# Attention, mixing layer and top-2 attention experts in one kernel: float32 exponentials for the first six pairs of heads

## The chip, the cores and the metric

One core of a Trainium2 chip runs the whole kernel in one launch. The metric is device time in microseconds (us), from the profiler, median of several executions; less is better. The engines are TensorE (PE for matrix products, PEld for its weight loads), VectorE (DVE), ScalarE (ACT), GpSimd (POOL) and SyncE (SP, which issues nearly all DMAs).

## The reference, cut to what matters

Three layers follow each other, for 4 batches, sequence 576, 8 heads of 64. Only the first, a decayed causal attention, and the start of the second are touched.

```python
scores = q @ k.T / 8 + cum[:, None] - cum[None, :]    # cum: running sum of log f; causal
attn = exp(scores - rowmax); attn /= attn.sum(-1) + 1e-9
x = attn @ v                                          # per head, laid out [batch, 576, 512]
u = x + (x.T @ U @ V).T                               # second layer
y = u + relu(u @ w_ch1) @ w_ch2
# third layer: four single-head attention experts over y, two of them chosen for each token
```

## The kernel before, in words

**Stages.** The attention stage handles 32 heads in 16 pairs (a pair is 128 of the 512 columns of x). It is followed by a dense stage (the products with w_ch1 and w_ch2, quarter by quarter of the weights) and by the stage of the experts. Some products of the dense stage's first quarter (the fills) are already mixed into the attention stage, from pair 5 on: PER_PAIR (line 45) says how many for each pair, and none belongs to pairs 0 to 4.

**Order.** The attention stage is a list of events, each with a due time: `put(h, us, do)` puts an event at `us` microseconds into the slot of head h (SLOT = 8.4), `early` puts it into the 15.6 before slot 0. The list is sorted by due time and issued in that order, and PE, DVE, ACT, POOL and SP each keep their part of that order (line 1299). The due times order the work; they don't time it.

**One head.** head_events (line 962) issues two sets of score products into two PSUM tiles (float32r, L267), exponentials of both on ACT (L287, three pieces of 576, 512 and 512 columns), a copy of each piece to float16 on ACT (high_part, L292) and the remainder to float16 on DVE (low_part, L295). One slot later (due at 4.55) `attend` multiplies: weighted_values (L323, L325, L327) takes 15 blocks of 128x128, each with three float16 products (high exponential with high v, high with low v, low with high v), with a column of ones behind v that yields the row sums. row_scales (L372, L375) and normalise (L389) on DVE finish the head.

**Row maxima.** max_events (line 996) runs two heads ahead: in the slot of head h PE makes the rows of head h+2 (last_rows L184 into `ua`, first_rows_of L202 into `ub`), DVE takes maxima (last_max L189, then first_max L210 in four pieces), and in the next slot PE turns them (turn_max L216), ACT scales them (put_row L222) and a DMA puts them as row 127 into the head's q (L226). Score tiles, `ua` and `ub` share two PSUM buffers (tag s2) in the order: first scores, second scores, ua, ub.

**Values.** value_events (line 1033) reads v of a pair (load_v L818, one DMA), finds a power of two near its largest value (L333, L338, L345 to L347, L353, L358) and splits v into float16 high (ACT, L362) and low (DVE, L365).

**Filler products.** `busy` (line 1255) issues products of a constant with itself (L1258) that nobody reads: 8, 14 and 8 of them in each slot of heads 0 to 9.

**Other work in the slots.** split_high, split_moves and split_low (lines 820 to 862) cut q and k of a pair into high and low parts, two pairs ahead; the second head's halves are moved between partitions by DMA. mix_events (line 1116) makes u of a finished pair in odd slots: mix_sums (L873, plain float32 products), a copy on ACT (L877), mix_low on DVE (L880), two turns on PE (L890, L892), a copy and a store of u to DRAM (L897, L921). Weights of the first quarter are unpacked in slots 4 to 13.

**Before slot 0.** FIRST_SPLITS (line 1082) gives the due times of the splits of pairs 0 and 1; the moves of head 0 and the load of pair 1 stand ahead of the moves of head 1.

**Start of the dense stage.** For batches 1 and 2, ffn_begin (line 606), ffn_begin_high and ffn_begin_low fetch and cut u in the attention stage. For batch 3, `ffn_prepare(NC * (B - 1))` (line 1369) runs at the start of the dense stage: a DMA reads u (L629), ACT and DVE cut it (L652, L653).

Of the kernel before, what the change touches and what calls it, by code (L numbers as in the profile page):

```python
# [42 lines left out]
SLOT = 8.4  # L43
FIRST = 15.6
PER_PAIR = (0,) * 5 + (3, 3, 3, 3, 4, 4, 4, 4, 3, 3, 2)

# [18 lines left out]
def kernel(  # L65
# [44 lines left out]
    nc.gpsimd.memset(every[:], 1.0)  # L110
    spread = const.tile([P, P], BF16, name="spread")
    nc.gpsimd.memset(spread[:], 1.0 / VEXP)
    ars = []
# [123 lines left out]
    def exponent_tiles(pl_, n, eng=nc.gpsimd):  # L237

        made = []
        for i in range(n):  # L240
            two = pl_.tile([P, 2 * 1600 + 64], F16, name=f"ph{i}")
            eng.memset(two[:, 3200:3264], 0.0)
            made.append((two, two[:, 1600:3264]))
        return made
# [52 lines left out]
    def scores(hb, exps, select=False):  # L297

        ph, pl = exps
# [12 lines left out]
        return ph, pl  # L312

    def weighted_values(ph, pl, vh, vl, its=(0, NT), av=None):
# [26 lines left out]
    def value_power(at_):  # L341
# [3 lines left out]
        nc.vector.tensor_reduce(ar, at_[:], AX.X, OP.max)  # L345
        nc.vector.tensor_scalar(ar, ar, 1.0e-30, None, OP.max)
        nc.vector.tensor_scalar(ar.bitcast(I32), ar.bitcast(I32), 0x7F800000, None,  # L347
# [3 lines left out]
    def value_spread(full):  # L351
        rp = psf.tile([P, 1], F32, name="rsp", tag="f")
        nc.tensor.matmul(rp[:], spread[:], full[:].bitcast(BF16)[:, 1:2], start=True, stop=True)  # L353
        return rp
# [13 lines left out]
    def row_scales(av, rs):  # L368

        den = small.tile([P, NT], F32, name="den")  # L370
        total = av()[:, :, 64:65].rearrange("p t o -> p (t o)")
        nc.vector.tensor_scalar(den[:], total, 1.0e-9 * PSCALE, rs()[:, 0:1], OP.add, OP.mult)  # L372
        yield
# [425 lines left out]
    khigh = att.tile([P, S], F32R, name="khigh")  # L799
    vhs = []  # L800
    for i in range(2):
        vh_ = hpool.tile([P, 2, NT, 65], F16, name=f"vh{i}")
        vl_ = hpool.tile([P, 2, NT, 64], F16, name=f"vl{i}")
        nc.vector.memset(vh_[:, :, :, 64:65], 1.0)
        vhs.append((vh_, vl_))
    NPAIR = B * NP
# [26 lines left out]
    def split_moves(p, j):  # L833

        if p >= NPAIR:
            return
        qa, qb, ka, kb = pair_heads(p)[j]
        src = f32(chl[2 * p + j:2 * p + j + 1]) if p < 2 else cdram[2 * p + j]
        nc.sync.dma_start(f32(ka[64:66, 0:S]), src)
        if p == j == 0:  # L840
            load_qk(1)
        if j == 0:
            nc.sync.dma_start(f32(qb[lo_, :]), f32(qa[lo_, :]))
            nc.sync.dma_start(f32(kb[hi_, :S]), f32(ka[lo_, :S]))
        else:
            nc.sync.dma_start(f32(qa[lo_, :]), f32(qb[hi_, :]))
            nc.sync.dma_start(f32(ka[lo_, :S]), f32(khigh[hi_, :]))
            nc.sync.dma_start(f32(kb[lo_, :S]), f32(khigh[hi_, :]))

# [112 lines left out]
    def head_events(h):  # L962

        p, j = divmod(h, 2)
        hb = pair_heads(p)[j]
        ph, pl = exps[h % 2]
        st = {}
# [4 lines left out]
        def exp_(n):  # L972
            u, view = (0, 0) if n == 0 else (1, n - 1)
            view, o0, n_, _ = score_views(st[u], u)[view]
            st["pf", n] = exponentials(view, n_), o0, n_
# [9 lines left out]
        def attend():  # L985
            vh, vl = vhs[p % 2]
            st["av"] = weighted_values(ph, pl, vh[:, j], vl[:, j])

        put(h + 1, 4.55, attend)
        finish = row_scales(lambda: st["av"], lambda: st_rs[p])  # L990
        for us in (6.15, 6.35):
            put(h + 1, us, lambda: st.update(rn=next(finish)))
        put(h + 1, 6.55, lambda: normalise(places[p % 2][2][:, :, j * D:j * D + D], st["av"],
                                           st["rn"]))

    def max_events(h):
# [13 lines left out]
        if h < 2:  # L1010
            for us, n in ((8.5, 0), (8.7, 1)) if h == 0 else ((12.3, 0), (13.2, 1)):
                early(us, rows, n)
            early((9.2, 12.9)[h], lambda: last_max(st[0], st["mx"]))
            for n, t in enumerate((3, 2, 1, 0)):
                early((9.8, 13.7)[h] + 0.6 * n, first, t)
        else:
# [16 lines left out]
    def value_events(p):  # L1033
# [11 lines left out]
        vh, vl = vhs[p % 2]  # L1045
        if p == 0:
            early(6.6, step, "am", None, value_max)
            early(11.7, step, "amt", "am", value_turn)
            early(13.9, step, "full", "amt", value_power)
            early(14.9, step, "rp", "full", value_spread)  # L1050
            put(0, 0.2, factor)
            put(0, 4.95, lambda: value_high(vr, st_rs[p], vh))
            put(0, 8.0, lambda: value_low(vr, st_rs[p], vh, vl))
            return
        put(h, 1.95, step, "am", None, value_max)
        put(h, 4.54, step, "amt", "am", value_turn)
# [6 lines left out]
    def split_events(p):  # L1063
# [15 lines left out]
        put(2 * (p - 2) - 1 if p > 2 else 0, 0.1, load_qk, p)  # L1079
        put(2 * (p - 2), 2.0 if p > 2 else 8.1, load_v, p)  # L1080

    FIRST_SPLITS = ((5.8, 6.5, 7.5), (7.1, 8.8, 10.3), (11.6, 14.7, 14.8), (13.2, 19.3, 19.2))

    def first_events():
# [5 lines left out]
        def table():  # L1090
            one_ = small.tile([1, 1], F32, name="one", bufs=1)
            nc.scalar.activation(one_[:], vhs[0][0][0:1, 0, 0, 64:65], AF.Ln)

# [191 lines left out]
    put(10, 4.6, read_late)  # L1285
    for b in (1, 2):
        put(8 * b + 8, 4.0, ffn_begin, b)
# [592 lines left out]
```

## Time and profile before

| | us |
|---|---|
| median of 3 runs (819.69 to 822.27) | 821.81 |
| the profiled execution | 822.43 |
| its span, from the first to the last instruction | 820.4 |
| PE busy in the span | 765.5 (93%) |
| DVE busy | 626.0 (76%) |
| ACT busy | 450.6 (55%) |
| mean granted TensorE clock | 0.991 |

Busy time is a union of intervals: a PE that is busy by the table can still be issuing slower than it could. "Idle before" in a row is the time in which the engine did nothing ahead of that instruction, with what ended it. In a row of the timeline, several like instructions in sequence are merged: the first number is the start, the second the time to the end of the last one.

### The profile page before, as it was taken

The numbers are of one execution on the slowest core, as the hardware profiler recorded it, in microseconds if no ns is written. First come the engines' busy times: TensorE is split into PE (matmuls) and PEld (weight loads), VectorE is DVE, ScalarE is ACT, GpSimd is POOL, SyncE is SP. The second block draws the span as 40 slices with busy tenths as digits, with TensorE's granted clock in tenths as the row PEclk, the third lists the DMA queues.
The fourth block names the chain that finished last, engine by engine and source line by source line (L and its number), as shares of the span: only waits on it lengthen the run. The fifth ranks groups of instructions, "written<-read, shape, count | busy, mean of one in ns | idle before, by whom it ended". The sixth has DMA issues, their size and how long they took to land.

```text
span 820.4 us, 19717 instructions
## 1 busy us (share of the span) xinstructions
PE 765.5 (93%) x7726; PEld 659.4 (80%) x7726; DVE 626.0 (76%) x1716; ACT 450.6 (55%) x895; POOL 148.3 (18%) x248
## 2 busy tenths in 40 slices
PE   3898889999999989998999999999999999889997
PEld 2788889999999989876777777777778887768764
DVE  6899999999999839979773685467436798877874
ACT  6778887877787615627231232113212666566674
POOL 9542433324232000000010000000001411010110
PEclk9999999999999999999999999999999999989999
DMA  6466665666564154854033234200101433122222
GB/s 187 133 188 177 179 194 147 188 185 172 168 173 131 58 168 152 278 161 157 34 116 97 79 95 160 81 1 1 59 30 37 124 96 91 43 76 57 51 82 81
DMA packets 59212, 96.10 MB, mean 117 GB/s; under 512 B 4928, under 2 KB 39088, under 8 KB 59120
## 3 DMA queue, kind: packets, MB, share of 16 engines
q1 hardware_dynamic: 56864, 90.78, 37.3%
q10 hardware_dynamic: 2256, 4.06, 1.4%
q8 instruction: 61, 1.00, 0.5%
q14 instruction: 31, 0.25, 0.1%
HBM read 53.25 MB, written 23.74 MB: 94 GB/s over the span
## 4 chain that ended last, share of the span: by engine, by line
PE 46%; DVE 7%; issue 2%; DMA 2%; ACT 1%; POOL 0%; SPq 0%; POOLq 0%
PE cps L678 15%; PE hps L662 14%; PE pq L1522 4%; PE pv L1574 3%; PE po L1608 3%; PE sc L267 2%; PE ub L202 1%; DMA yst<-ydram 1%; DVE ph L295 1%; PE av L323 1%; PE av L327 1%; DVE ub L210 1%; DVE w16a L519 1%; PE av L325 1%; DMA ust<-udram 1%
## 5 line engine op out<-in xcount | busy, mean ns | idle before, releaser
L667 ACT ACTIVATE hh<-hps 128x288 f16<-128x288 f32 (+1 forms) x128 | 52.6, 411 | 218.4 <-PE hps L662 192.9
L668 DVE SCALAR_TENSOR_TENSOR hl<-hps,hh 128x288 f16<-128x288 f32 (+1 forms) x128 | 58.1, 454 | 81.4 <-ACT hh L667 80.9
L210 DVE CUSTOM_DVE_ANT_0 ub<-ub,maskm 128x448 f32<-128x448 f32 x192 | 82.1, 427 | 9.6 <-PE ub L202 7.8
L267 PE MATMUL sc<-qa,ka 128*128 128x288 f32 (+4 forms) x288 | 73.8, 315 | 3.2 <-DVE mx L189 1.7
L323 PE MATMUL av<-vh,ph 128*128 128x65 f16 x720 | 71.9, 196 | 0.0
L325 PE MATMUL av<-vl,ph 128*128 128x64 f16 x720 | 71.7, 194 | 0.0
L327 PE MATMUL av<-vh,ph 128*128 128x65 f16 x720 | 71.6, 194 | 0.0
L684 DVE SCALAR_TENSOR_TENSOR yc<-cps,back,yc 128x288 f32<-128x288 f32 x96 | 49.3, 514 | 25.3 <-PE cps L678 22.4
L323 PEld LDWEIGHTS <-ph 128*128 128x128 f16 x720 | 66.6, 98 | 1.1 <-issue 0.4
L325 PEld LDWEIGHTS <-ph 128*128 128x128 f16 x720 | 66.6, 99 | 0.9
L327 PEld LDWEIGHTS <-ph 128*128 128x128 f16 x720 | 66.7, 98 | 0.0
L267 PE MATMUL sc<-qb,kb 128*128 128x288 f32 (+4 forms) x288 | 64.4, 305 | 0.0
L287 ACT ACTIVATE aside<-sc 128x512 f32<-128x512 f32 (+1 forms) x75 | 45.3, 617 | 24.4 <-PE sc L267 22.4
L295 DVE TENSOR_TENSOR ph<-aside,ph 128x512 f16<-128x512 f32 (+1 forms) x75 | 55.1, 746 | 1.7 <-ACT ph L292 1.7
L267 PEld LDWEIGHTS sc<-qa,ka 128*128 128x128 f32 x288 | 49.9, 193 | 7.6 <-issue 2.2
L295 DVE TENSOR_TENSOR ph<-pf,ph 128x512 f16<-128x512 f32 (+1 forms) x69 | 48.8, 712 | 9.1 <-ACT ph L292 8.8
L267 PEld LDWEIGHTS sc<-qb,kb 128*128 128x128 f32 x288 | 53.3, 192 | 1.6
L189 DVE CUSTOM_DVE_ANT_0 ua<-ua,maskm 128x576 f32<-128x576 f32 x48 | 36.4, 759 | 16.6 <-PE ua L184 16.4
L678 PE MATMUL cps<-hh,w16b 128*128 128x288 f16 x256 | 48.3, 286 | 0.8 <-DVE hl L668 0.8
L678 PE MATMUL cps<-hh,w16a 128*128 128x288 f16 x256 | 48.4, 286 | 0.0
L678 PE MATMUL cps<-hh,w1lf 128*128 128x288 f16 x256 | 48.3, 286 | 0.0
L662 PEld LDWEIGHTS <-w16a 128*128 128x128 f16 x384 | 37.4, 98 | 13.2 <-issue 3.8
(269 smaller groups left out, 2356.0 us busy)
## 6 DMA issues: line engine op xcount, KB each, us to landing
raw<-in_w_dram SPq DMA_DIRECT2D x32, 512.0 KB
ust<-udram SPq DMA_DIRECT2D x14, 576.0 KB
ydram<-yc SPq DMA_DIRECT2D x10, 576.0 KB
aside<-in_qk_dram SPq DMA_DIRECT2D x8, 576.0 KB
room<-in_qk_dram SPq DMA_DIRECT2D x8, 576.0 KB
udram<-ustage SPq DMA_DIRECT2D x16, 288.0 KB
ydram<-ust SPq DMA_DIRECT2D x8, 576.0 KB
yc<-ydram SPq DMA_DIRECT2D x8, 576.0 KB
```

What stands on the lines that cost most here:

```text
L210: nc.vector.tensor_tensor_reduce(ub[:, bk, off:off + w], ub[:, bk, off:off + w], maskm[:, S - w:S], 1.0, NEG, OP.add, OP.max, mx[:, t:t + 1])
L267: nc.tensor.matmul(ps[:, bk, off:off + w], wa, xa, start=bk not in banks[:n], stop=bk not in banks[n + 1:])
L287: nc.scalar.activation(pf[:, 0:S].rearrange("p (c n) -> p c n", c=2) if whole else pf[:, 0:n], view, AF.Exp, scale=ISC)
L295: nc.vector.tensor_tensor(pl[:, o0:o0 + n], pf[:, 0:n], ph[:, o0:o0 + n], OP.subtract)
L323: nc.tensor.matmul(av[:, it, :], ph[:, c:c + P], vh[:, jt, :], start=first, stop=False)
L325: nc.tensor.matmul(av[:, it, 0:64], ph[:, c:c + P], vl[:, jt, :], start=False, stop=False)
L327: nc.tensor.matmul(av[:, it, :], pl[:, c:c + P], vh[:, jt, :], start=False, stop=last)
L662: nc.tensor.matmul(ph[:], wa[:, k, fs], xa[:, k], start=n == 0, stop=n == 3 * KT - 1)
L667: after(lambda: nc.scalar.activation(hh[:], ph[:], AF.Relu), lambda: nc.vector.scalar_tensor_tensor(hl[:], ph[:], 0.0, high, OP.max, OP.su ...
L668: lambda: nc.vector.scalar_tensor_tensor(hl[:], ph[:], 0.0, high, OP.max, OP.subtract))
L678: nc.tensor.matmul(pc[:], wa[:, t, dsl], xa[:], start=n == 0, stop=n == 3 * FT - 1)
L684: nc.vector.scalar_tensor_tensor(yc[:, d, :], pc[:], back, yc[:, d, :], OP.mult, OP.add)
```

## The change

- The first six pairs (NPLAIN = 6, heads 0 to 11) keep their exponentials in float32: ACT writes them into one tile, the copies to float16 and the DVE remainders are gone, and `attend` makes one plain float32 product for each of the 15 blocks (128 columns of weights, 65 columns of v with its ones). It is due at 2.0 instead of 4.55 in its slot, the three steps behind it at 3.9 to 4.1.
- For these pairs v isn't split; two DMAs bring its two heads into place (rows of 64 in 65 columns), due later.
- Filler products: 4 and 8 in each slot of heads 0 to 9 instead of 8, 14 and 8.
- Before slot 0: the second head's moves (head 1) come ahead of the load of pair 1 and of the moves of head 0; the splits of pair 1 and head 1's row maxima have other due times, and the row of head 0 goes over ACT.
- ffn_begin and its two steps run for batch 3 too, in the slots behind the last head.

The exponents' float16 tile and the float32 one share storage, as do the two forms of v; a constant tile of 1/8192 is replaced by a factor in an existing instruction. The diff, cut to its core:

```diff
+NPLAIN = 6
...
+            one_ = pl_.tile([P, 1664], F32, name=f"ph{i}")
+            eng.memset(one_[:, 1600:1664], 0.0)
+            two = one_[:].bitcast(F16)
+            made.append((two, two[:, 1600:3264], one_))
...
+    def plain_values(whole, vw, av=None):
+        if av is None:
+            av = ps1.tile([P, NT, 65], F32, name="av")
+        for it in range(NT):
+            order = list(range(it + 1)) if it < NT - 1 else [0, 4, 1, 2, 3]
+            for jt in order:
+                c = J_OFF[jt] + (it - jt) * P
+                nc.tensor.matmul(av[:, it, :], whole[:, c:c + P], vw[:, jt, :],
+                                 start=jt == order[0], stop=jt == order[-1])
+        return av
...
     def load_v(p):
-        if p < NPAIR:
+        if p < NPLAIN:
+            for a in range(2):
+                nc.sync.dma_start(vws[p % 2][:, a, :, 0:64], v[p // NP, p % NP][:, a])
+        elif p < NPAIR:
             nc.sync.dma_start(places[p % 2][1], v[p // NP, p % NP])
...
+        if j == 2:
+            qa, qb, ka, kb = pair_heads(p)[0]
+            nc.sync.dma_start(f32(qb[lo_, :]), f32(qa[lo_, :]))
+            nc.sync.dma_start(f32(kb[hi_, :S]), f32(ka[lo_, :S]))
+            return
...
+        nc.sync.dma_start(f32(qa[lo_, :]), f32(qb[hi_, :]))
+        nc.sync.dma_start(f32(ka[lo_, :S]), f32(khigh[hi_, :]))
+        if p == 0:
+            rows()
+            load_qk(1)
+            split_moves(0, 2)
+        nc.sync.dma_start(f32(kb[lo_, :S]), f32(khigh[hi_, :]))
...
+            if plain:
+                to = whole[:, o0:o0 + n_]
+                nc.scalar.activation(to if u else to.rearrange("p (c n) -> p c n", c=2), view,
+                                     AF.Exp, scale=ISC)
...
+            if plain:
+                continue
             put(h, th, lambda n: high_part(ph, *st["pf", n]), n)
             put(h, tl, lambda n: low_part(ph, pl, *st["pf", n]), n)
...
-        put(h + 1, 4.55, attend)
+        put(h + 1, 2.0 if plain else 4.55, attend)
...
-            for us, n in ((8.5, 0), (8.7, 1)) if h == 0 else ((12.3, 0), (13.2, 1)):
+            for us, n in ((8.5, 0), (8.7, 1)) if h == 0 else ((11.3, 0), (12.3, 1)):
...
-            early(12.6, lambda: put_row(hb, st["mt"]))
+            early(12.6, lambda: put_row(hb, st["mt"], True))
...
+        if p < NPLAIN:
             return
...
-        put(2 * (p - 2), 2.0 if p > 2 else 8.1, load_v, p)
+        put(*((2 * p - 2, 4.6) if p < NPLAIN else (2 * (p - 2), 2.0)), load_v, p)
-    FIRST_SPLITS = ((5.8, 6.5, 7.5), (7.1, 8.8, 10.3), (11.6, 14.7, 14.8), (13.2, 19.3, 19.2))
+    FIRST_SPLITS = ((5.8, 6.5, 7.5), (7.1, 7.8, 10.3), (13.0, 14.7, 14.8), (14.2, 19.3, 19.2))
...
-        put(h, 0.54, busy, 8)
-        put(h, 2.1, busy, 14)
-        put(h, 3.9, busy, 8)
+        put(h, 0.54, busy, 4)
+        put(h, 4.4, busy, 8)
...
-    for b in (1, 2):
+    for b in (1, 2, 3):
         put(8 * b + 8, 4.0, ffn_begin, b)
```

## Rows read from the trace of the kernel before

**Rows 1.** Windows cut at first scores of heads 2, 8, 10, 14; last columns: clock, DMA.

```profile
core 0: us, PE busy (x) PEld busy (x) DVE busy (x) ACT busy (x) POOL busy (x), PEclk, DMA share, GB/s
34.84:101.70 66.86, 58.82 (x869) 55.15 (x870) 62.62 (x182) 55.69 (x111) 25.61 (x19) 1.00 0.60 171
101.70:137.57 35.87, 32.11 (x388) 30.39 (x387) 33.47 (x97) 29.89 (x62) 11.40 (x8) 1.00 0.60 172
84.25:101.70 17.45, 14.83 (x220) 13.81 (x219) 16.70 (x48) 15.20 (x31) 6.09 (x5) 1.00 0.60 175
```

**Rows 2.** Groups by line, 34.84 to 101.70 (eight heads): busy, mean ns | idle before.

```profile
L295 DVE TENSOR_TENSOR ph<-aside,ph 128x512 f16<-128x512 f32 (+1 forms) x19 | 14.5, 774 | 0.0
...
L295 DVE TENSOR_TENSOR ph<-pf,ph 128x512 f16<-128x512 f32 x5 | 3.4, 683 | 0.0
...
L365 DVE SCALAR_TENSOR_TENSOR vl<-room,rs,vh 128x640 f16<-128x640 f32 x2 | 1.8, 876 | 0.0
```

**Rows 3.** PE's timeline in one pair: start, us, instruction [idle before <- what ended it].

```profile
71.85 0.76 PE L202 MATMUL ub<-ka,qa 127*128 127x448 f32 x4 [0.70 <-ACT pf L287]
...
74.92 0.40 PE L267 MATMUL sc<-qa,ka 128*128 128x288 f32 x1 [0.83 <-DVE mx L189]
...
77.33 0.27 PE L216 MATMUL mt<-ident,mx 128*5 128x128 f32 x1 [1.11 <-DVE mx L210]
```

**Rows 4.** Timelines of PE and PEld: one attend (first, last), fillers, plain float32, loads.

```profile
40.87 0.19 PE L323 MATMUL av<-vh,ph 128*128 128x65 f16 x1
...
42.21 0.19 PE L327 MATMUL av<-vh,ph 128*128 128x65 f16 x1
...
81.01 0.62 PE L1258 MATMUL some<-every 128*128 128x128 bf16 x8
...
46.73 1.28 PE L873 MATMUL gp<-aside,ut 128*96 128x128 f32 x10
...
46.68 0.25 PEld L873 LDWEIGHTS gp<-aside,ut 128*96 128x96 f32 x2
...
47.75 0.30 PEld L184 LDWEIGHTS ua<-ka,qa 127*128 127x128 f32 x2
```

**Rows 5.** DVE's timeline behind one attend and its row maxima.

```profile
74.05 0.76 DVE L189 CUSTOM_DVE_ANT_0 ua<-ua,maskm 128x576 f32<-128x576 f32 x1
...
74.72 0.66 DVE L210 CUSTOM_DVE_ANT_0 ub<-ub,maskm 128x448 f32<-128x448 f32 x1
...
76.27 0.21 DVE L372 TENSOR_SCALAR den<-av,rs 128x5 f32<-128x5 f32 x1
...
76.89 0.23 DVE L210 CUSTOM_DVE_ANT_0 ub<-ub,maskm 128x64 f32<-128x64 f32 x1
...
77.04 0.48 DVE L389 TENSOR_TENSOR aside<-av,rn 128x320 f32<-128x320 f32 x1
```

**Rows 6.** The start: PE's timeline, and SP's issue of one move.

```profile
14.77 0.82 PE L184 MATMUL ua<-ka,qa 127*128 127x288 f32 x2 [2.06 <-DMA ka<-khigh]
...
17.86 0.58 PE L267 MATMUL sc<-qa,ka 128*128 128x288 f32 x1
...
19.09 1.06 PE L1258 MATMUL some<-every 128*128 128x128 bf16 x8
...
24.32 0.62 PE L1258 MATMUL some<-every 128*128 128x128 bf16 x8
...
10.23 0.54 SPq L847 DMA_DIRECT2D ka<-khigh  x1
```

**Rows 7.** PE's timeline: the first scores of head 2.

```profile
34.84 0.37 PE L267 MATMUL sc<-qa,ka 128*128 128x288 f32 x1 [1.09 <-DMA qa<-mr]
```

**Rows 8.** Start of the dense stage: timelines of SP, ACT and PE, and one window.

```profile
296.57 0.60 SPq L629 DMA_DIRECT2D ust<-udram  x1
...
300.85 1.24 ACT L652 CAST uh<-ust 128x576 fp32r<-128x576 f32 x2 [3.23 <-DMA ust<-udram]
...
302.91 0.16 PE L464 MATMUL rsp<-ar,every 128*128 128x1 bf16 x1 [2.43 <-DVE ar L459]
...
303.87:307.28 3.41, 3.41 (x16) 3.41 (x16) 2.19 (x9) 0.00 (x0) 0.00 (x0) 0.50 0.92 301
```

More of the change, by code (lines that the diff above doesn't have):

```diff
@@ L110 @@
     nc.gpsimd.memset(every[:], 1.0)
-    spread = const.tile([P, P], BF16, name="spread")
-    nc.gpsimd.memset(spread[:], 1.0 / VEXP)
     ars = []
@@ L240, in exponent_tiles @@
         for i in range(n):
-            two = pl_.tile([P, 2 * 1600 + 64], F16, name=f"ph{i}")
-            eng.memset(two[:, 3200:3264], 0.0)
-            made.append((two, two[:, 1600:3264]))
+            one_ = pl_.tile([P, 1664], F32, name=f"ph{i}")
+            eng.memset(one_[:, 1600:1664], 0.0)
+            two = one_[:].bitcast(F16)
+            made.append((two, two[:, 1600:3264], one_))
         return made
@@ L352, in value_spread @@
         rp = psf.tile([P, 1], F32, name="rsp", tag="f")
-        nc.tensor.matmul(rp[:], spread[:], full[:].bitcast(BF16)[:, 1:2], start=True, stop=True)
+        nc.tensor.matmul(rp[:], every[:], full[:].bitcast(BF16)[:, 1:2], start=True, stop=True)
         return rp
@@ L371, in row_scales @@
         total = av()[:, :, 64:65].rearrange("p t o -> p (t o)")
-        nc.vector.tensor_scalar(den[:], total, 1.0e-9 * PSCALE, rs()[:, 0:1], OP.add, OP.mult)
+        if rs() is None:
+            nc.vector.tensor_scalar(den[:], total, 1.0e-9 * PSCALE, None, OP.add)
+        else:
+            nc.vector.tensor_scalar(den[:], total, 1.0e-9 * PSCALE, rs()[:, 0:1], OP.add, OP.mult)
         yield
@@ L799 @@
     khigh = att.tile([P, S], F32R, name="khigh")
-    vhs = []
+    vhs, vws = [], []
     for i in range(2):
[L802 to L805, printed above, removed]
+        v_ = hpool.tile([P, 2 * NT * 65], F32, name=f"vw{i}")
+        vws.append(v_[:].rearrange("p (a t d) -> p a t d", a=2, t=NT))
+        nc.vector.memset(vws[i][:, :, :, 64:65], 1.0)
+        n0, n1 = 2 * NT * 65, 2 * NT * (65 + 64)
+        vhs.append((v_[:].bitcast(F16)[:, 0:n0].rearrange("p (a t d) -> p a t d", a=2, t=NT),
+                    v_[:].bitcast(F16)[:, n0:n1].rearrange("p (a t d) -> p a t d", a=2, t=NT)))
     NPAIR = B * NP
@@ L836, in split_moves, with rows @@
             return
+        if j == 2:
[3 more added lines that the diff above has]
+            return
         qa, qb, ka, kb = pair_heads(p)[j]
         src = f32(chl[2 * p + j:2 * p + j + 1]) if p < 2 else cdram[2 * p + j]
-        nc.sync.dma_start(f32(ka[64:66, 0:S]), src)
-        if p == j == 0:
-            load_qk(1)
+        def rows():
+            nc.sync.dma_start(f32(ka[64:66, 0:S]), src)
         if j == 0:
+            rows()
+            if p == 0:
+                return
             nc.sync.dma_start(f32(qb[lo_, :]), f32(qa[lo_, :]))
             nc.sync.dma_start(f32(kb[hi_, :S]), f32(ka[lo_, :S]))
[L845 to L848, printed above, removed]
+            return
+        if p:
+            rows()
+        nc.sync.dma_start(f32(qa[lo_, :]), f32(qb[hi_, :]))
+        nc.sync.dma_start(f32(ka[lo_, :S]), f32(khigh[hi_, :]))
+        if p == 0:
+            rows()
+            load_qk(1)
+            split_moves(0, 2)
+        nc.sync.dma_start(f32(kb[lo_, :S]), f32(khigh[hi_, :]))
     def split_low(p, j, which=(0, 1)):
@@ L965, in head_events @@
         hb = pair_heads(p)[j]
-        ph, pl = exps[h % 2]
+        ph, pl, whole = exps[h % 2]
+        plain = p < NPLAIN
         st = {}
@@ L974, in exp_ @@
             view, o0, n_, _ = score_views(st[u], u)[view]
-            st["pf", n] = exponentials(view, n_), o0, n_
+            if plain:
+                to = whole[:, o0:o0 + n_]
+                nc.scalar.activation(to if u else to.rearrange("p (c n) -> p c n", c=2), view,
+                                     AF.Exp, scale=ISC)
+            else:
+                st["pf", n] = exponentials(view, n_), o0, n_
         put(h, 0.0, products, 0)
@@ L985, in attend @@
         def attend():
+            if plain:
+                st["av"] = plain_values(whole, vws[p % 2][:, j])
+                return
             vh, vl = vhs[p % 2]
             st["av"] = weighted_values(ph, pl, vh[:, j], vl[:, j])
-        put(h + 1, 4.55, attend)
-        finish = row_scales(lambda: st["av"], lambda: st_rs[p])
-        for us in (6.15, 6.35):
+        put(h + 1, 2.0 if plain else 4.55, attend)
+        finish = row_scales(lambda: st["av"], lambda: st_rs.get(p))
+        for us in (3.9, 4.0) if plain else (6.15, 6.35):
             put(h + 1, us, lambda: st.update(rn=next(finish)))
-        put(h + 1, 6.55, lambda: normalise(places[p % 2][2][:, :, j * D:j * D + D], st["av"],
+        put(h + 1, 4.1 if plain else 6.55, lambda: normalise(places[p % 2][2][:, :, j * D:j * D + D], st["av"],
                                            st["rn"]))
@@ L1010, in max_events @@
         if h < 2:
-            for us, n in ((8.5, 0), (8.7, 1)) if h == 0 else ((12.3, 0), (13.2, 1)):
+            for us, n in ((8.5, 0), (8.7, 1)) if h == 0 else ((11.3, 0), (12.3, 1)):
                 early(us, rows, n)
-            early((9.2, 12.9)[h], lambda: last_max(st[0], st["mx"]))
+            early((9.2, 12.45)[h], lambda: last_max(st[0], st["mx"]))
             for n, t in enumerate((3, 2, 1, 0)):
-                early((9.8, 13.7)[h] + 0.6 * n, first, t)
+                early((9.8, 13.1)[h] + 0.6 * n, first, t)
         else:
@@ L1045, in value_events @@
         vh, vl = vhs[p % 2]
[L1046 to L1053, printed above, removed]
+        if p < NPLAIN:
             return
+        if p < NPLAIN + 2:
+            put(h + 1, 6.0, lambda: nc.vector.memset(vh[:, :, :, 64:65], 1.0))
         put(h, 1.95, step, "am", None, value_max)
```

6 lines of the change are left out of this document (3 added, 3 removed).

## The prediction

> **What bounds the kernel now.** I read the busy shares first and then, because they average over stages, the windows of the attention stage cut at the first scores of heads 2, 10 and 14 [rows 1]. In heads 2 to 9 DVE is busy 62.6 of 66.9 us; PE shows 58.8, yet part of that is filler products that nobody reads. PE's waits say the same [rows 3]: in the pair of heads 6 and 7 it waits 0.83 and 1.11 us for DVE's row maxima and 0.70 for exponentials, 2.64 in all. So DVE bounds these slots, and the reader should see in the groups [rows 2] what the change takes from it. From head 10 on PE carries fills and no fillers, and waits less. Last I read the start, the wait at head 2 and the start of the dense stage [rows 6, 7, 8].
>
> **What DVE and ACT lose.** The remainders take 14.5 + 3.4 us in eight heads, 4.5 us per pair; with the low part of v at 0.88 and the search for its largest value about as long, DVE loses some 6 of the 16.7 us it works in a pair of 17.45 [rows 1, 2]. ACT loses its copies. Neither engine then bounds the slot, so what happens to PE decides.
>
> **What PE gains.** An attend is now 45 float16 products whose starts run from 40.87 to 42.21, 1.37 us in all [rows 4]. After the change it is 15 plain float32 products. Such products exist in the trace: five of them, 128 columns wide, appear as ten loads and ten matmuls in 1.28 us, 0.11 us for each of two passes per product, and there the moving side sets the pace. With 65 columns the moving side of a pass falls to 0.055. The weights do not shrink: two loads of 96 float32 columns stand 0.25 - 0.163 = 0.084 us apart, two loads of 128 float32r columns 0.30 - 0.19 = 0.11 [rows 4]. No row shows a plain float32 load of 128 columns. The bounds are 0.055 (load wholly hidden) and 0.16 (each load also waits for the matmul of the one before to start, 0.05 after its own load in L873's two rows, 46.68 and 46.73); I take 0.11, because 0.084 x 128/96 gives the same, and both spacings are of loads that nothing held up. Thirty passes make 3.3 us, 1.93 more per head.
>
> The Trainium skill (FP8 and Floating Point Precision, TensorE Precision Notes) says that true float32 takes four passes through the array. If each brought its own load, an attend would take 6.6 us and the sum would rise by another 40. The trace agrees with four only in streaming time (0.11 us for 128 columns is two column times per pass) and shows two loads, so that reading gets no chance.
>
> Eighteen fillers of 0.056 us go from each slot of heads 0 to 9 (eight in 0.62, the last 0.22 long [rows 4]): 1.0 us per head.
>
> **Pairs 1 to 4.** PE's own work in a pair is 17.45 - 2.64 = 14.8 [rows 1, 3]. Adding 2 x 1.93 and taking off 2.0 gives 16.7. To that come waits that I follow along DVE [rows 5]. When an attend ends, DVE needs about 1.0 for denominator, reciprocal and normalisation, including the wait for the result, then 0.87 for the last rows' maximum, which frees the buffer of the next first scores; PE has 1.4 of other work (ua, ub, eight fillers), so it waits 0.5. The four maxima end 1.6 after that; PE has one score set and four fillers, 0.8, so the turn waits 0.65. In odd slots the turns of u wait 0.7 for DVE's g, queued behind a maximum. That is 1.85; none is the other bound, and I take 1.3, as the slow first product behind a wait is already in the 14.8. A pair then takes 18.0, four take 72.0 against 66.86 [rows 1]: **+5.1**. The gain on DVE is bought with PE time that is just as scarce.
>
> **Heads 10 to 12.** Three slots hold the attends of heads 9 to 11 and no fillers: +5.8. The wait for exponentials (up to 1.0) and some 0.7 of the wait for maxima go: **+4.1** on 35.87.
>
> **The start.** Head 1's row maxima start at 14.77 because the move of its k, issued at 10.23 behind the 576 KB load of pair 1 and head 0's moves, lands late [rows 6]. Issued about 8.3 and ahead of that load, it lets them start near 11, and the second half waits only for head 0's maxima. Head 0's own moves pass behind the load, but its scores need them only when the row with its maxima has landed, whose DMA keeps its place. First scores come near 15.6 instead of 17.86: -2.3. Putting that row over ACT instead of DVE costs nothing while ACT waits for pair 1. The wait of 1.09 before head 2 [rows 7] may go too, as v of pair 2 no longer stands ahead of its DMA on SP. Against that, eight fillers take 1.06 us at 19.09 and 0.62 at 24.32 [rows 6]: TensorE runs at its lower clock until about 24 us. Fewer fillers come then, and the first plain attend, due from about 25 us, costs 6.6 at that clock. I take **-1.8** at head 2, between -4.3 and +1.5.
>
> **v's DMAs and the moves.** Two issues instead of one per pair, and they wait on SP for the last attend that reads the old v; behind them stand moves for a head two slots away and the next row of maxima, more than half a slot off. The cover is that slack; without it the next head's scores would wait about 1 us, as in [rows 7]. POOL keeps its order and loses a memset.
>
> **Dense stage.** The read of u for batch 3 is issued at 296.57 and ACT waits 3.23 us for it; behind ACT stands DVE's cut, behind that a small reduction, and PE waits 2.43 for it; then PE works 3.41 us at the lower clock [rows 8], a loss of 1.7. With three quarters of u read some ten us earlier, and the last quarter taken from the tile on chip, all this goes: **-4.1**. The bounds are 0 (the read waits for the store of pair 14 and SP stands still behind it) and -4.1. Next late there would be the reads of batches 0 and 1, issued right behind.
>
> **Sum.** -1.8 + 5.1 + 4.1 - 4.1 = +3.3 on the profiled execution's 822.4, 825.7. That execution stands 0.6 above the median of 821.8, so the forecast is **825.1**. A measurement can tell about 0.3% from no change: faster is under 819.3, slower over 824.3.
>
> **Rivals.**
> - *Loads hide* (0.055 a pass; the other end, 0.16, would give 18 more, 843, and shares the chance of the clock's case): 1.65 less per head, 20 us in twelve heads, of which DVE's chain of maxima gives back a quarter: about 810. For it: loads overlap matmuls. Against: the two spacings of [rows 4]. Chance 0.12.
>
> - *PE never waits* and the start gives its best: -5.2 in pairs 1 to 4 and -2.5 at the start against the forecast, about 817. For it: DVE and ACT lose a third of their work. Against: the chain of [rows 5] is untouched. Chance 0.15.
> - *The clock stays low*: with fillers gone, PE may not rise from its lower level before the plain attends, whose passes move columns half of the time. Each slot at that level costs about 5 us; to head 3 that is 834, to head 9 near 890. It decides if the first rise comes later than about 30 us. For it: the lower clock until 24 us with fillers, and the drop at 303.87 after one wait of 2.43 [rows 6, 8]. Against: slots of heads 6 to 9, with waits, stayed at the full clock [rows 1]. The Trainium skill (TensorE: Matmul & The Clock Gate, Part 1) says that the throttled state is the default and activity releases it; the trace agrees (1.06 against 0.62 us for the same eight products). Chance 0.2.
> - *The early u does nothing*: 829. Chance 0.05.
>
> **How the numbers follow.** The forecast keeps 0.48, with its own range of 820 to 830. Faster: 0.12 + 0.10 from the second rival + 0.03 of the forecast = 0.25. Same: 0.05 + 0.18 = 0.23. Slower: 0.27 + 0.2 + 0.05 = 0.52. The range leaves out the first rival and the long end of the third: 815 to 834.
>
> **What would show it.** In the changed kernel plain loads of 128 columns 0.11 us apart and attends of 3.3; DVE near 60% in heads 2 to 9 and pairs of 18; PE waiting for maxima still; first scores near 15.6; no wait and no drop of the clock near 303. Pairs under 16 or attends under 2.5 would make the prediction wrong, and so would a lower clock past head 1.

## The result and the profile after

The changed kernel takes **825.36 us** (824.68 to 826.42 in four runs) against 821.53 for the kernel before: ratio 1.0053, 95% interval 1.0028 to 1.0079. It is slower, by about half a per cent, and the forecast of 825.1 was met. The profiled execution took 825.63 with a span of 823.9 us (before: 820.4). The total is closer than its terms, as the stages of the profiled executions show. Each is cut at first scores; positive is slower.

| stage | before | after | measured | forecast |
|---|---|---|---|---|
| start to head 2 | 34.84 | 32.58 | -2.26 | -1.8 |
| heads 2 to 9 (pairs 1 to 4) | 66.86 | 74.26 | +7.40 | +5.1 |
| heads 10 to 13 | 35.87 | 40.87 | +5.00 | +4.1 |
| heads 14 to 30 | 140.42 | 140.60 | +0.18 | 0 |
| head 31, dense stage | 360.65 | 356.93 | -3.72 | -4.1 |
| experts' stage to the end | 181.76 | 178.66 | -3.10 | 0 |
| span | 820.4 | 823.9 | +3.5 | +3.3 |

The windows of the changed kernel that answer to [rows 1] and to the last of [rows 8], with the experts' stage; the columns are those of [rows 1]:

```profile
core 0: us, PE busy (x) PEld busy (x) DVE busy (x) ACT busy (x) POOL busy (x), PEclk, DMA share, GB/s
32.58:106.84 74.26, 65.44 (x597) 61.97 (x597) 42.48 (x135) 40.33 (x82) 22.84 (x18) 1.00 0.55 153
106.84:147.71 40.87, 37.68 (x343) 36.20 (x342) 28.94 (x87) 26.64 (x55) 11.13 (x8) 1.00 0.54 151
306.00:330.00 24.00, 24.00 (x184) 23.70 (x183) 18.61 (x48) 10.35 (x19) 0.00 (x0) 1.00 0.39 126
645.24:823.90 178.66, 162.62 (x1727) 130.82 (x1724) 140.55 (x431) 113.99 (x235) 28.55 (x105) 0.99 0.29 78
```

DVE's work falls from 62.62 to 42.48 us in eight heads and ACT's by 15; PE's busy time went up by 6.6 though 144 of its 240 filler products were gone, and the stretch grew by 7.4. That is a bottleneck handed from one engine to another. Around 306 us PE is busy without a gap at the full clock: the wait and the lower clock of [rows 8] are gone.

PE's waits from head 2 to head 13 (the turn of the maxima for the four maxima, the turns of u for g, the first scores for the last rows' maximum; 12.5 us in all), the first plain attend on PE's timeline, and all attends by their line (duration in ns, minimum, median, maximum):

```profile
engine line waited for: us in total, times, longest us
PE mt L215 <- DVE mx L209: 5.9, 7, 0.9
PE up L926 <- DVE g L914: 4.1, 5, 1.5
PE sc L267 <- DVE mx L188: 2.5, 5, 0.6
```

```profile
27.20 3.51 PE L339 MATMUL av<-vw,ph 128*128 128x65 f32 x30
```

```profile
L339 PEld LDWEIGHTS av<-vw,ph x360: 190/192/192, 27.1 to 134.4; 128*128 128x128 f32 x180
L339 PE MATMUL av<-vw,ph x360: 275/275/276, 27.2 to 134.5; 128*128 128x65 f32 x180
```

The 180 products are 360 loads and 360 matmuls, so 30 passes an attend. The next instruction begins at 30.52: 3.32 us, 0.111 a pass, where the prediction took 3.3 and 0.11.

One regular pair, heads 4 and 5, on PE and then on DVE (start, duration, instruction, idle time before it and its releaser):

```profile
59.49 0.40 PE L267 MATMUL sc<-qa,ka 128*128 128x288 f32 x1 [0.45 <-DVE mx L188]
...
61.45 0.27 PE L215 MATMUL mt<-ident,mx 128*5 128x128 f32 x1 [0.86 <-DVE mx L209]
...
62.85 3.51 PE L339 MATMUL av<-vw,ph 128*128 128x65 f32 x30
...
67.24 0.52 PE L183 MATMUL ua<-ka,qa 127*128 127x288 f32 x2
...
69.57 0.39 PE L926 MATMUL up<-vs,g 128*128 128x256 f32 x1 [0.63 <-DVE g L914]
```

```profile
66.40 0.17 DVE L385 TENSOR_SCALAR den<-av 128x5 f32<-128x5 f32 x1 [3.73 <-PE av L339]
...
67.79 0.77 DVE L188 CUSTOM_DVE_ANT_0 ua<-ua,maskm 128x576 f32<-128x576 f32 x1 [0.47 <-PE ua L183]
```

These rows are from the slot of head 5, in which PE attends for head 4. Read the two engines against each other. DVE stands idle for 3.73 us while PE attends, then for 0.47 until PE has made the score rows `ua`; after that PE waits for the maxima taken from them. They take turns. The pair (52.02 to 70.27) is 18.25 us long, of which 0.45 + 0.86 + 0.63 = 1.94 are PE's waits, so PE's own work is 16.3.

### The profile page after: what moved, and what is told of

Its sections match the earlier page's. It is cut to its first block, busy times and chain, and to the rows that moved or that the text cites. A ratio compares the mean times of both kernels' runs of the same rounds, so it can differ in the third digit from the quotient of the medians.

```text
span 823.9 us, 18857 instructions
## 1 busy us (share of the span) xinstructions
PE 774.2 (94%) x7354; PEld 668.9 (81%) x7354; DVE 595.8 (72%) x1645; ACT 428.0 (52%) x854; POOL 145.0 (18%) x247
## 4 chain that ended last, share of the span: by engine, by line
PE 45%; DVE 8%; ACT 1%; DMA 1%; issue 1%; POOL 0%; SPq 0%; ACTq 0%; DVEq 0%; POOLq 0%
PE cps L693 15%; PE hps L677 14%; PE pq L1561 4%; PE pv L1613 3%; PE po L1647 2%; PE sc L267 2%; PE ub L201 1%; DVE ub L209 1%; DVE ph L295 1%; DMA ust<-udram 1%; DVE w16a L534 1%; PE av L323 1%; DVE qb L1576 1%; PE av L327 1%; PE av L325 1%
## 5 line engine op out<-in xcount | busy, mean ns | idle before, releaser
L323 PEld LDWEIGHTS <-ph 128*128 128x128 f16 x540 | 49.6, 97 | 1.1 <-issue 0.4
L325 PEld LDWEIGHTS <-ph 128*128 128x128 f16 x540 | 49.5, 98 | 0.8
L295 DVE TENSOR_TENSOR ph<-pf,ph 128x512 f16<-128x512 f32 (+1 forms) x61 | 42.9, 708 | 9.4 <-ACT ph L292 9.2
L327 PEld LDWEIGHTS <-ph 128*128 128x128 f16 x540 | 49.6, 97 | 0.0
L677 PEld LDWEIGHTS <-w16a 128*128 128x128 f16 x384 | 37.4, 98 | 13.5 <-issue 4.1
L693 PEld LDWEIGHTS <-w16b 128*128 128x128 f16 x384 | 37.6, 98 | 10.6 <-issue 1.1
L677 PEld LDWEIGHTS <-w1hf 128*128 128x128 f16 x384 | 37.4, 98 | 9.5
L677 PEld LDWEIGHTS <-w16b 128*128 128x128 f16 x384 | 36.9, 98 | 9.9 <-issue 0.5
L693 PEld LDWEIGHTS <-w1lf 128*128 128x128 f16 x384 | 37.3, 98 | 9.4
L693 PEld LDWEIGHTS <-w16a 128*128 128x128 f16 x384 | 37.2, 98 | 9.5 <-issue 0.2
```

What stands on the lines that cost most here:

```text
L295: nc.vector.tensor_tensor(pl[:, o0:o0 + n], pf[:, 0:n], ph[:, o0:o0 + n], OP.subtract)
L323: nc.tensor.matmul(av[:, it, :], ph[:, c:c + P], vh[:, jt, :], start=first, stop=False)
L325: nc.tensor.matmul(av[:, it, 0:64], ph[:, c:c + P], vl[:, jt, :], start=False, stop=False)
L327: nc.tensor.matmul(av[:, it, :], pl[:, c:c + P], vh[:, jt, :], start=False, stop=last)
L677: nc.tensor.matmul(ph[:], wa[:, k, fs], xa[:, k], start=n == 0, stop=n == 3 * KT - 1)
L693: nc.tensor.matmul(pc[:], wa[:, t, dsl], xa[:], start=n == 0, stop=n == 3 * FT - 1)
```

## The experiments

Line numbers differ by a few between kernels. All times are medians; on the three occasions on which these runs were made the kernel before had 821.45, 822.06 and 822.34. Timelines and windows are of one profiled execution each.

**Early u alone**, on the kernel before:

```diff
-    for b in (1, 2):
+    for b in (1, 2, 3):
```

> The kernel before with one line of the change: the last batch's u is prepared and read during the heads, like that of batches 1 and 2. Theory: the waits and the stretch at the lower clock at the start of the dense stage go and nothing else moves, so about 3.7 us less than the kernel before (in the changed kernel the way from head 31's first scores to those of the experts' stage is 356.9 us against 360.7), near 817.8. Rival (the early u does nothing by itself, since its read waits for the store of pair 14): the time of the kernel before, 821.5.

Measured: 817.54 us, ratio 0.9935 (0.9914 to 0.9956). As the theory has it: the way from head 31 to the experts' stage is 356.66 us, 3.99 less than before. The profile is not equal in all the rest: heads 2 to 13 took 2.3 us longer than in the kernel before, with a stretch at the lower clock and a wait for a DMA. One line of the change is worth 4 us, and the changed kernel hides that gain.

**Start and early u**, on the kernel before: that line, and the changed `split_moves`, FIRST_SPLITS, due times of head 1's maxima and row over ACT.

```diff
-            for us, n in ((8.5, 0), (8.7, 1)) if h == 0 else ((12.3, 0), (13.2, 1)):
+            for us, n in ((8.5, 0), (8.7, 1)) if h == 0 else ((11.3, 0), (12.3, 1)):
```

> As the run with the early u alone, and the start of the changed kernel besides: the order of the first moves, the times of head 1's row maxima, the row of maxima over ACT. Exponentials and values stay as before. Theory: head 1's maxima start over 2 us sooner because its moves are sooner, so first scores of head 2 come 2 us sooner than before and the whole takes about 815.5. Rival: the start gained because the value events of pair 0 left DVE and ACT; then the moves alone give under 0.7 us and the time is 817 or more. An answer to whether the plain products pay at all stands in the same number: if this is below the kernel before by 5 or more, they cost about 10 us.

Measured: **816.07 us**, ratio 0.9926 (0.9902 to 0.995), the best version of this study; it keeps the split products. Head 1's maxima start at 11.48 and the first scores of head 2 come at 32.17; with the early u alone they came at 34.41. PE's timelines, first of that run, then of this:

```profile
34.41 0.37 PE L267 MATMUL sc<-qa,ka 128*128 128x288 f32 x1 [1.37 <-DMA qa<-mr]
```

```profile
32.17 0.37 PE L267 MATMUL sc<-qa,ka 128*128 128x288 f32 x1 [0.87 <-DMA qa<-mr]
```

So the new start brings the 2.2 us with pair 0's value events still there; which of its parts does, the moves or the due times, was not tested. In the medians of the two runs the step is 1.5, with intervals that overlap; the traces carry it, not the ratio. What is left between this run and the changed kernel, 9.3 us in the medians, is the price of the plain products with all that goes with them: fillers, due times, loads of v. The traces put it in heads 2 to 13: 103.49 us here, 115.13 in the changed kernel, of which an experts' stage that is 1.7 us shorter there hides a part. Windows of this run, heads 2 to 9 and 10 to 13:

```profile
32.17:99.24 67.07, 58.75 (x868) 55.20 (x869) 62.34 (x183) 56.01 (x112) 26.02 (x20) 1.00 0.60 171
99.24:135.66 36.42, 32.33 (x388) 30.42 (x387) 33.48 (x97) 30.06 (x62) 11.28 (x8) 1.00 0.60 170
```

**Twice the columns**, on the changed kernel: does the load set the pace of a product?

```diff
-                nc.tensor.matmul(av[:, it, :], whole[:, c:c + P], vw[:, jt, :],
+                wide = 2 if it < NT - 1 else 1
+                nc.tensor.matmul(av[:, it:it + wide, :], whole[:, c:c + P], vw[:, jt:jt + wide, :],
```

> The changed kernel; ten of an attend's fifteen plain products (those of the first four blocks of rows) take 130 columns of v instead of 65, the second 65 into a block that the next group overwrites, so the output stays the same and the loads too. Theory (two loads of 128 float32 columns, 0.11 us each, set a product's pace and the columns run beside them): an attend stays at 3.3 to 3.5 us and the time at 825 to 828. Rival (the moving columns set it, at 0.055 us per 65 of them and pass): 20 x 0.055 = 1.1 us more per attend, 13 in twelve heads, 838 or more.

Measured: 826.26 us, 0.9 above the changed kernel. The attend of the pair above on PE's timeline:

```profile
62.98 3.51 PE L340 MATMUL av<-vw,ph 128*128 128x130 f32 x30
```

Same length with twice the columns in 20 of 30 passes, so up to 130 columns are free here. That the loads set the pace is what remains, and their spacing in [rows 4] was 0.11 already. The Trainium skill (FP8 and Floating Point Precision, TensorE Precision Notes) counts four passes for true float32; the trace shows two loads and two matmuls for each product, and 130 columns fit in the 0.11 us of a load, which leaves room for two column times per pass but not for four loads.

**Upper halves**, on the changed kernel: one load for each product instead of two. The lower 16 bits of exponentials and values are left out of the computation.

```diff
-                nc.tensor.matmul(av[:, it, :], whole[:, c:c + P], vw[:, jt, :],
+                nc.tensor.matmul(av[:, it, :], upper(whole[:, c:c + P]), upper(vw[:, jt, :]),
...
+        return ap.bitcast(BF16).rearrange("p (n two) -> p n two", two=2)[:, :, 1]
```

> The changed kernel, its plain products reading only the upper 16 bits of each exponential and each value (bfloat16 operands, so the lower bits of both are left out of the computation); same number of products, same columns, same waits. Theory (two float32 loads of 128 columns set an attend's 3.32 us): an attend falls to 0.5 to 0.8 us, PE loses 2.6 us in each of twelve heads, DVE's chain gives back about a third of it, and the time comes to about 803. If the attends' length came through whole it would be 793 to 795. Rival (DVE's chain or the wait for exponentials sets the slots, and the attends' length lies beside it): no shorter than 818.

Measured: 802.96 us, 22.4 less than the changed kernel. The edit halves the size of the operands as well as the number of loads: a product with its one load costs 0.033 us instead of 0.22. An attend and what follows it on PE:

```profile
51.77 0.66 PE L342 MATMUL av<-vw,ph 128*128 128x65 bf16 x15
52.27 1.31 PE L910 MATMUL gp<-room,ut 128*96 128x128 f32 x10
```

0.50 instead of 3.32 us: 2.82 x 12 = 34 us less work on PE, of which 22.4, two thirds, reach the end, as forecast. The rest went into waits and, as the window of heads 2 to 9 shows, a stretch at the lower clock:

```profile
29.77:88.96 59.19, 48.39 (x477) 43.65 (x478) 42.87 (x135) 40.64 (x84) 25.33 (x20) 0.91 0.72 199
```

So the attends lie on the path of the changed kernel; the rival, that something else sets its slots, is out (the rival's bound was 818).

**Normalise late**, on the changed kernel: on DVE the next maxima go ahead of denominator, reciprocal and normalisation.

```diff
-        for us in (3.9, 4.0) if plain else (6.15, 6.35):
+        for us in (6.45, 6.5) if plain else (6.15, 6.35):
...
-        put(h + 1, 4.1 if plain else 6.55, lambda
+        put(h + 1, 6.55, lambda
```

> The changed kernel with the denominator, reciprocal and normalisation behind the next maxima on DVE instead of ahead of them; PE, ACT, POOL and SP keep their order. Theory (in the prediction: when an attend ends DVE first spends about 1.0 us on these three, and only then takes the last rows' maximum, for which PE's next scores wait): the waits for the last maximum go, those for the four maxima and for g shrink by up to 1.0 each, together 7 to 10 of the 12.5 us that PE waited for DVE between 30 and 145 us, so 816 to 819. Rival (these waits are PE's slack, and the slots are set by PE's own 16.7 us or by the exponentials): under 2 us, 823.5 or more.

Measured: 824.58 us, 0.8 less. My theory fell. PE's waits from head 2 to 13:

```profile
engine line waited for: us in total, times, longest us
PE mt L215 <- DVE den L385: 6.3, 7, 1.1
PE up L926 <- DVE g L914: 4.1, 5, 1.5
```

The 2.5 us for the last maximum are gone and a pair is 0.4 shorter (17.85), but the others stay (the row names the denominator because it now stands right behind the maxima). DVE's timeline in the slot shown above:

```profile
66.39 0.77 DVE L188 CUSTOM_DVE_ANT_0 ua<-ua,maskm 128x576 f32<-128x576 f32 x1 [4.30 <-PE ua L183]
```

DVE now idles 4.30 us in one piece. The maximum starts 8.30 us into the slot of head 5 in either kernel (67.79 behind 59.49, 66.39 behind 58.09). In this slot DVE was not kept from the maxima by the normalisation but by the score rows that PE makes behind its attend; the 0.4 us came from the pair's other slot.

**Attend later**, on the changed kernel: attend at 4.55, behind the score rows, the three steps at 6.15 to 6.55.

```diff
-        put(h + 1, 2.0 if plain else 4.55, attend)
+        put(h + 1, 4.55, attend)
```

> The changed kernel with the plain attend, its denominator, reciprocal and normalisation at the times in the slot that the split attend had: PE makes the score rows for the maxima first and attends while DVE takes the maxima. Theory (PE's own work of 16.7 us per pair, and on top of it waits for DVE's chain from the attend's end over normalisation and last maximum to the turn): the waits for the last rows' maximum and for the four maxima shrink from about 1.2 us in an even slot to under 0.4, and heads 2 to 13 take 4 to 8 us less, 818 to 822 in all. Rival (the waits only move: PE waits for exponentials or for the values' normalisation instead): within 2 us of the changed kernel, 823.5 to 827.5.

Measured: 823.56 us, 1.8 less than the changed kernel and on the rival's side. The mechanism is the theory's all the same: PE's waits for DVE, 12.5 us in the changed kernel, are all gone, and 5.0 for exponentials take their place:

```profile
PE ub L201 <- ACT ph L1012: 3.2, 5, 0.9
PE ua L183 <- ACT ph L1012: 1.8, 2, 0.9
```

Windows of heads 6 and 7 and of heads 8 and 9:

```profile
67.15:84.97 17.82, 16.33 (x152) 15.48 (x150) 11.18 (x36) 11.33 (x24) 5.61 (x4) 1.00 0.68 174
84.97:107.40 22.43, 20.96 (x151) 20.16 (x150) 11.18 (x36) 11.42 (x24) 5.60 (x4) 0.77 0.58 159
```

PE's timeline: the attend in the first slot of either pair, and what came ahead of the second:

```profile
72.58 3.52 PE L339 MATMUL av<-vw,ph 128*128 128x65 f32 x30
...
88.24 0.53 PE L183 MATMUL ua<-ka,qa 127*128 127x288 f32 x2 [0.90 <-ACT ph L1012]
89.34 0.76 PE L201 MATMUL ub<-ka,qa 127*128 127x448 f32 x4 [0.57 <-ACT ph L1012]
...
90.39 6.53 PE L339 MATMUL av<-vw,ph 128*128 128x65 f32 x30
```

The same instructions with the same waits take 4.6 us longer in the second pair, because the clock fell to its lower level (1.2 GHz) and the attend with it. The mean clock of all ten runs is 0.989 to 0.991 (the changed kernel: 0.995 to 0.998), so something like it happens each time. The waits moved from a place with fillers to one without.

**Attend later, waits filled**: the same with the fillers moved into those waits.

```diff
-        put(h, 4.4, busy, 8)
+        put(h, 3.6, busy, 14)
+        put(h, 3.9, busy, 9)
```

> The run with the attend later, with its fillers placed where its trace shows PE waiting for exponentials (14 ahead of ua where it waited 0.9, 9 between ua and ub where it waited 0.57) and none behind ub. Theory: that kernel lost 2.96 + 1.65 us in the slots of heads 8 and 9 at the lower clock after these waits (11.71 and 10.72 against 8.75 and 9.07 for heads 6 and 7), and eight fillers on PE's path in each of ten heads; with the clock at its full level throughout, 814 to 819. Rival 1 (the clock falls for the plain products themselves, not for the waits ahead of them): it falls again, 820 or more. Rival 2 (fillers push the score rows back, so that DVE's maxima come late): the clock stays up, but the waits for maxima return, 820 to 824.

Measured: 819.27 us, 4.3 less than without, ratio to the kernel before 0.9977 (0.9959 to 0.9994); 0.3 above the range that I gave. The clock stays up in heads 2 to 13:

```profile
31.30:103.43 72.13, 71.56 (x718) 68.47 (x718) 39.71 (x135) 40.19 (x83) 23.80 (x18) 1.00 0.59 162
103.43:141.20 37.77, 37.28 (x344) 36.08 (x342) 27.41 (x86) 26.54 (x55) 9.82 (x7) 1.00 0.55 156
```

PE is busy 71.56 of 72.13 us, with one wait of 0.3 in heads 2 to 13, and still needs five more than the kernel before [rows 1]. That one had 30 fillers a head, so these are not the difference: 8.0 us of PE's idle time are down to 0.6, and the attends alone add 8 x 1.95 = 15.6. Both rivals fall in this profile. There are more fillers than in the changed kernel (27 a head, not 12) and in other places, so no run tells which of the two keeps the clock. Of the versions with float32 products in six pairs this is the best, and the run with the start and the early u alone is 3 us below it.

**No fillers**, on the changed kernel: the loop over ten heads is taken out.

```diff
-    for h in range(10):
-        put(h, 0.54, busy, 4)
-        put(h, 4.4, busy, 8)
```

> The changed kernel without any fillers in heads 0 to 9. Theory (four of them lie in the wait for the four maxima and eight in that for the last maximum, so they cost little, and the plain attends keep the clock up): 823 to 826. Rival (the prediction's third: without fillers the clock rises later or falls during the plain attends): each slot at the lower level costs 3 to 5 us, 830 or more.

Measured: 842.48 us, ratio 1.0241 (1.0195 to 1.0287). This is the prediction's third rival, up to head 3. The first three attends on PE:

```profile
28.72 6.61 PE L339 MATMUL av<-vw,ph 128*128 128x65 f32 x30
...
42.09 6.61 PE L339 MATMUL av<-vw,ph 128*128 128x65 f32 x30
...
55.00 6.61 PE L339 MATMUL av<-vw,ph 128*128 128x65 f32 x30
```

All are at the lower level; the slots of heads 1 to 3 take 13.6, 13.1 and 16.5 us where the changed kernel has 8.5, 8.6 and 10.8, which is 15.3 of the 17.1 us lost. In the slots from head 4 on an attend is 3.5 us long again (3.92 once, behind a stretch at the lower clock near 112 us, which makes head 9's slot 1.5 longer), and the pairs that begin at heads 4 and 6 (18.05, 18.14) are 0.1 to 0.2 shorter than with fillers: there these cost next to nothing.

**Fillers in heads 0 and 1 alone**, on the changed kernel:

```diff
-    for h in range(10):
+    for h in range(2):
```

> The changed kernel with its fillers in heads 0 and 1 alone. Theory (without any, three attends ran at the lower clock, 6.61 us each, and once the clock was up it stayed so with one exception: the fillers are needed for the first rise, and later ones lie in waits): the clock rises near 26 us as in the changed kernel and the time is 823 to 828. Rival (fillers are needed in every slot, or the clock falls back at the next waits): the slots of heads 2 to 4 at the lower level again, 835 or more.

Measured: 836.92 us, ratio 1.0189. My theory fell again. The clock rises in time for the first attend (3.52 us at 26.78) and falls for the next two. Windows of heads 2 to 4:

```profile
34.89:55.00 20.11, 19.30 (x91) 18.56 (x90) 3.50 (x13) 4.54 (x9) 3.58 (x3) 0.50 0.32 88
55.00:68.41 13.41, 11.47 (x81) 10.95 (x81) 6.41 (x22) 7.22 (x15) 5.62 (x4) 0.86 0.43 116
```

PE is busy 19.30 of 20.11 us in the first window, and the clock stays at its lower level (0.50) throughout. Without their fillers the slots of heads 2 and 3 take 12.25 and 16.70 us (8.61 and 10.83 in the changed kernel). From head 4 on the slots are about as long as with fillers or a little shorter, but for head 9's, 1.5 longer, with a stretch at the lower clock near 107 us.

**All fillers of before**, on the changed kernel:

```diff
-        put(h, 0.54, busy, 4)
-        put(h, 4.4, busy, 8)
+        put(h, 0.54, busy, 8)
+        put(h, 2.1, busy, 14)
+        put(h, 3.9, busy, 8)
```

> The changed kernel with the fillers of the kernel before (8, 14 and 8 products per head instead of 4 and 8). Theory (PE's own work sets the slots of heads 2 to 9, so what is put ahead of its score rows comes through, and what is put ahead of the wait for the four maxima does not): 14 x 0.056 = 0.8 us in each of ten heads and little else, 831 to 835. Rival (DVE's chain sets them): under 2 us more, up to 827.5.

Measured: 835.26 us, ratio 1.017. 9.9 more than the changed kernel: 18 x 0.056 = 1.0 us in each of ten heads, whole. That is just past my range: I had the four ahead of the wait for the maxima hidden, and nothing in the sum is.

**Half plain**: pair 0 plain, of pairs 1 to 5 the first head only, 6, 8 and 6 fillers.

```diff
-        plain = p < NPLAIN
+        plain = p < NPLAIN or p < NHALF and j == 0
```

> Only the first head of each of the pairs 1 to 5 goes plain (and both of pair 0); the second head keeps its float16 halves and its value events, on that head's values alone; attends at their old place behind the score rows, 20 fillers per head. Theory (split attends make DVE the bound, 16 us of work per pair, plain ones PE, 16.3 per pair; with one of each PE has 14 and DVE 13, and neither waits long for the other): pairs 1 to 4 take 15 to 16 us each, heads 10 to 13 some 2 us less than in the changed kernel, 810 to 816 in all. Rival (it is not the sum of work but the order of the chain PE, DVE, PE in each slot that sets the pitch, and both kinds pay their own): 817 or more.

Measured: 822.46 us, no different from before (0.9989 to 1.0028). Heads 4 and 5, then head 7's slot, then heads 8 and 9:

```profile
52.05:67.68 15.63, 15.28 (x185) 14.55 (x183) 11.78 (x41) 11.87 (x25) 5.61 (x4) 1.00 0.67 194
75.62:89.31 13.69, 12.48 (x92) 12.04 (x93) 8.17 (x31) 7.46 (x15) 3.29 (x3) 0.75 0.61 166
89.31:108.09 18.78, 15.70 (x185) 14.67 (x183) 15.50 (x45) 13.48 (x28) 6.10 (x4) 1.00 0.61 162
```

The first is the time that I wanted, 15.63, and it beats nothing: the same pair took 15.44 with split products and the new start, and DVE has only 11.78 us of work in it. The second lost about 4 us at the lower clock, so the total says less than it seems. The third answers for this form at the full clock: 18.78 us, where split products take 17.46 and plain ones 18.33. PE works 15.70 of them and waits 3.1, of which 2.5 are for DVE's maxima. The theory fell: PE and DVE have less than 16 us of work each, and their waits for each other set the pitch, as the rival has it.

## Why the prediction was right, and where it was not

**Attend.** Right to the digit: 3.32 for 3.3. The trace excludes both ends (0.111 a pass, not 0.055 and not 0.16), and the run with twice the columns shows that the columns don't set it. One difference in the working, 0.25 - 0.163, is 0.087 by the figures as written, not 0.084; scaled to 128 columns that is 0.116, and the choice stands. DVE lost 5.0 us a pair (20.14 in four) where some 6 were taken, which bounds nothing.

**Pairs 1 to 4.** Own work 16.3 for 16.7, waits 1.94 in a regular pair for 1.3, so 18.25 for 18.0. The step that failed is the choice between the bounds, "none is the other bound, and I take 1.3": the waits came out just past the upper bound of 1.85. And pair 1 was taken like the others; PE waits for the four maxima in the slot of head 2 as well (0.86), which has no turns of u ahead of it, and the pair takes 19.44. Together +2.3. The mechanism was placed wrong, too: I followed DVE's queue from the end of the attend and made the normalisation's 1.0 us the cause. Taking it away gave 0.4 a pair; moving the attend behind the score rows took away every wait for DVE. The order on PE, attend first and score rows behind it, made them, not the length of DVE's queue.

**Heads 10 to 13.** +5.0 for +4.1: PE's busy time rose by 5.57, close to the 5.8 that I added. The term that failed is the 1.7 us of waits that I took off: PE's idle time fell only from 3.76 to 3.19. The waits for exponentials went, and 1.5 us for g came in their place, beside 1.6 for the four maxima. With the attend later this stretch takes 37.77 us instead of 40.87.

**Start.** -2.26 for -1.8. Head 1's maxima start at 11.48, as expected, but first scores come at 16.52, not 15.6: PE waits 2.45 us for the DMA of head 0's row. PE's timeline:

```profile
16.52 0.58 PE L267 MATMUL sc<-qa,ka 128*128 128x288 f32 x1 [2.45 <-DMA qa<-mr]
...
32.58 0.40 PE L267 MATMUL sc<-qa,ka 128*128 128x288 f32 x1 [0.60 <-DVE mx L188]
```

So the first scores come 1.34 us sooner than before, not 2.3. The slot of head 1 made up for it: it is 0.91 shorter, although it holds a plain attend. The wait of 1.09 for a DMA at head 2 is gone (0.60 for DVE stands there), eighteen fillers are gone, and the first attend ran at the full clock (3.51 us), not at the 6.6 that the prediction priced for the lower clock.

**Dense stage.** -3.72 for -4.1; one line by itself gave the same (-3.99).

**What was not foreseen** is the experts' stage, 3.1 us shorter with the same instructions. Windows of its stretches at the lower clock, before and then after:

```profile
703.23:706.64 3.41, 2.97 (x14) 2.17 (x14) 2.63 (x14) 0.43 (x2) 0.00 (x0) 0.50 0.39 89
...
723.70:730.50 6.80, 6.21 (x61) 5.77 (x62) 6.29 (x19) 3.77 (x8) 0.87 (x2) 0.50 0.30 65
```

```profile
729.05:732.46 3.41, 2.94 (x13) 2.85 (x14) 3.28 (x8) 2.89 (x6) 0.86 (x2) 0.50 0.38 83
```

The stage lasts 178.6 to 178.7 us in the four profiled kernels with a single short stretch and no other (the changed kernel, twice the columns, waits filled, all fillers), 179.7 to 180.4 in the eight others of the experiments, which have two, a longer one, or one more at the end, and 181.76 in the kernel before, with a short one, a long one and 1.1 us at the end. What makes the stretches stays open. The changed kernel begins the stage 6.6 us later, but the run with the waits filled begins it at 638.15, half a microsecond from the kernel before, and has the short stage. Runs of one kernel differ nearly as much: of the kernel before, 26 with a mean clock of 0.992 average 822.1 us and nine with 0.997 average 819.6; where in these runs the clock fell is not on record. So the forecast was right in total by luck: +2.3 and +0.9 too little in the heads met 3.1 that nobody had counted. Against the runs at 0.997 the changed kernel's loss is nearer 6 us, an estimate (825.4 - 819.6).

**The rivals.** That loads hide and that PE never waits fell with the attend's length and the 12.5 us of waits; that the early u does nothing fell with the run that has it alone. That the clock stays low is no fancy: it is what the same change does without fillers, at the price I gave for a slot (5 us; measured 4.5 to 5.7). My sums from that price were off: to head 3 I had 834 where three slots made it 842, and "to head 9 near 890" does not follow from 5 us a slot, since the eight slots of heads 2 to 9 would make 40, or 865. In the profile of the changed kernel all twelve attends ran at the full clock, so the twelve fillers that it keeps were enough there.

## What to carry to other kernels

Before giving a bound engine's work to another, add it to that engine's own work in the same stage, and look at the order: an operation that grows from 1.4 to 3.3 us delays everything issued behind it, here the score rows for which the other engine waits. Price a matmul by its weight loads when the moving side is narrow, and test the parts of a mixed change singly: here one line was worth 4 us and the headline cost 9 or more. Fillers cost least in the engine's waits, and when the waits move, look again where the clock falls: here the same waits without fillers lost 4.6 us in a pair, and with more fillers, placed in them, nothing.

## What the runs showed of the hardware

- At the full clock a plain float32 product with 128 columns of weights costs 0.22 us on PE, two loads 0.11 apart, and 130 moving columns cost no more than 65 (an attend of 3.51 us with either). At the lower clock an attend takes 6.61.
- With fillers in heads 0 and 1 alone, PE was busy 19.30 of 20.11 us in the slots of heads 2 and 3, two plain float32 attends among its work, and the granted clock stayed at 0.50; in the changed kernel, with 12 bfloat16 fillers in each slot, the same slots ran at the full clock.
- The windows' granted clock can be wrong at the start of an execution: without fillers they show 1.00 for heads 1 to 3 while attends take 6.61 us instead of 3.51. There the level has to be read from durations.
